# A retention layer with routed experts: past products first, row stores on GpSimd, and the last stores split

## The chip, the cores and the metric

The kernel runs on one core of a Trainium2 chip. The core has five engines that run side by side, each with a queue of its own: TensorE (PE in the profile; PEld is its weight load), VectorE (DVE), ScalarE (ACT), GpSimd (POOL) and SyncE (SP), which here only issues DMAs. Sixteen DMA engines move data between the chip's memory and the core's SBUF. The metric is the device time of one execution in microseconds.

## The reference, cut to what matters

```python
# q, k, v: (8 batches, 8 heads, 576 tokens, 64), float32
scores = scale * q @ k.T
ret = scores * gamma[h] ** (t - s)        # for t >= s, else 0
x = (ret @ v) -> (8, 576, 512)            # heads side by side

logits = x @ w_gate                       # 8 experts
local = sigmoid(x @ w_local)
for b in batches:
    for s in tokens:
        e = argmax(logits[b, s]) if s == 0 or local[b, s] < 0.5 else e of the token before
        out[b, s] = softmax(logits[b, s])[e] * relu(x[b, s] @ w1[e]) @ w2[e]
...
```

The first half is a retention layer: causal attention without a softmax, whose weight decays with the distance. The second sends each token to one of eight experts (512 to 1024 to 512), where a token may take over the expert of the token before it.

## The kernel before, in words

**The retention stage.** The 4608 tokens (two sequences of 576 are nine chunks of 128) are handled in 36 chunks (NCH). A chunk's output has two parts: the products of its own masked scores with its values, and the products of its queries with the state that all earlier chunks of the sequence left. The state is a sum of key-value products, kept in PSUM (kv) and copied to SBUF after every chunk (states, two buffers). The chunk in the middle of a pair of sequences (MID) is half of the one and half of the other; the first chunk of a pair has no past.

The order on TensorE is written by hand (a manual schedule); for one step i of the loop it is: the scores of chunk i+1 (function scores, line 176), the outputs of chunk i (outputs: the value products, line 201, and then the past products, line 210), the state update of chunk i+1 (state, line 227), the gate products of chunk i-1 (rows, line 238), and the logits of chunk i-2 (logits, line 260), followed by a step of the routing when one is open. The other engines take the work in an order that the framework's scheduler chose. These matmuls use different parts of the TensorE array: scores contract over 64 rows into 128 columns (written 64*128), value products 128*64, past products 64*64, state updates 128*64 (64*64 in the middle chunk), gates 128*32, logits 128*128.

What the other engines do for a chunk: SyncE loads q, k and v in one DMA of 1 MB (ld, line 156, seven buffers) and, in between, pieces of the first expert's weights (line 162); DVE scales q (qT, line 165), masks the scores from PSUM into sT (line 180) and transposes the outputs in squares of 32 (x, line 247); POOL scales v (vs, line 169, four buffers) and writes one-hot lanes for the routing (line 187); ACT copies the outputs (xT, line 213), the state (line 230) and the gate products (line 241) out of PSUM. Each two chunks, four DMAs store the rows of x to a scratch tensor in memory (xd, line 250); in the kernel before they are issued by ACT. x has two buffers, each for two chunks. From xd the tokens are gathered later, expert by expert.

**The routing** (route) follows groups of 6 to 8 chunks on DVE and POOL, and ends some 30 us after the last chunk; TensorE fills part of this with tokens of expert 0 that are known early (block(-1)).

**The expert stage.** Tokens are sorted by expert into blocks of up to 768 tokens (GMAX = 6 groups of 128). For block j the function step(j) is run: POOL loads the weights of the next block and gathers its tokens (weights, load_tokens); a switch on the number of tokens (tc.Switch, for PE and ACT) picks one of the compiled variants of block(j, T). A block first does the first group of second-layer products of the block before it (first_group(j-1), line 683), then its own first layer (line 745), then the remainder in narrow pieces of 64 and 32 tokens (narrow), and then its groups 1, 2, 3 and so on (group, line 683, with ACT scaling each result into ys, line 687). Its own group 0 is left to the next step. After the switch POOL stores the results row by row with indirect DMAs (store, line 662): first group 0 of the block before, then groups 1 to 5 and the two narrow pieces (store_rest). A store that has no rows writes none but is still issued. NSURE is 9, so the steps that always run are 0 to 8, and with this data step 7 is the last with a block of its own; step 8 has only the first group of block 7 left, and its store.

Of the kernel before, what the change touches and what calls it, by code (L numbers as in the profile page):

```python
# [18 lines left out]
ET = mybir.EngineType  # L19
# [3 lines left out]
P = 128  # L23
B, H, S, DH = 8, 8, 576, 64
# [3 lines left out]
HP = H // 2  # L28
# [14 lines left out]
GMAX = TMAX // P  # L43
# [3 lines left out]
NSURE = E + 1  # L47

SIZES = [0, P] + list(range(2 * P, TMAX + 1, 32))
# [5 lines left out]
NARROW = (P // 2, P // 4)  # L55
# [7 lines left out]
def kernel(  # L63
# [10 lines left out]
    nc = tc.nc  # L74
# [44 lines left out]
    with ExitStack() as part:  # L119
# [70 lines left out]
        def outputs(i):  # L190
            m = i % PER
            g = chunks[i]
            qT, vs, sT = g["qT"], g["vs"], g["sT"]


            ops = ps_o.tile([P, 2, HP, P], F32, name="ops")
            for c in range(HP):
                for u in range(2):
                    r = slice((u ^ c & 1) * DH, ((u ^ c & 1) + 1) * DH)
                    h = 2 * c + u  # L200
                    nc.tensor.matmul(ops[r, c & 1, c // 2, :], lhsT=vs[:, h * DH:(h + 1) * DH], rhs=sT[:, u, c, :],  # L201
                                     start=(c < 2), stop=(m == 0), skip_group_check=True)
            if m > 0:

                n = HALF if m == MID else P
                for c in range(HP):
                    for u in range(2):
                        k = slice(u * DH, (u + 1) * DH)
                        r = slice((u ^ c & 1) * DH, ((u ^ c & 1) + 1) * DH)
                        nc.tensor.matmul(ops[r, c & 1, c // 2, 0:n], lhsT=states[(i + 1) % 2][k, c, :],  # L210
                                         rhs=qT[k, c, 0:n], start=False, stop=True, skip_group_check=True)
            g["xT"] = xT = work.tile([P, HP, P], F32, name="xT", bufs=2)
            nc.scalar.copy(xT.rearrange("p (a b) t -> p b a t", b=2), ops[:, :, 0:HP // 2])  # L213

# [17 lines left out]
        def rows(i):  # L232
            nonlocal x
            xT = chunks[i]["xT"]

            gps = ps_g.tile([P, P], F32, name="gps")
            for c in range(DK):
                nc.tensor.matmul(gps[c * SQ:(c + 1) * SQ, :], lhsT=gates[:, c, :], rhs=xT[:, c, :],
                                 start=True, stop=True, skip_group_check=True)
            parts = work.tile([P, P], F32, name="parts")  # L240
            nc.scalar.copy(parts, gps)
            chunks[i]["parts"] = parts


            if i % 2 == 0:
                x = work.tile([P, 2, NSQ, DK, SQ], F32, name="x", bufs=2)
            nc.vector.transpose(x[:, i % 2], xT.rearrange("p c (t s) -> p t c s", s=SQ))  # L247
            if i % 2:
                for a in range(NSQ):
                    nc.scalar.dma_start(  # L250
                        out=xd[(i - 1) * P:(i + 1) * P, a * P:(a + 1) * P].rearrange("(t s) d -> s t d", s=SQ),
                        in_=x[a * SQ:(a + 1) * SQ].rearrange("p b t c r -> p (b t) (c r)"))

# [200 lines left out]
        for M, at in ((P // 2, 0), (P // 4, 0), (P // 4, P // 2)):  # L454
            r = repeat[M, at] = table.tile([P, P], F32, name=f"repeat{M}_{at}")
# [12 lines left out]
        with tc.manual_schedule(engines={ET.PE}):  # L468
            for i in range(NCH + 2):
# [9 lines left out]
                if 0 <= i - 2:  # L479
# [3 lines left out]
                    if i - 2 in ends[:-1]:  # L483
                        k = ends.index(i - 2)
# [35 lines left out]
    narrow_ys = {M: later.tile([P, D * M // P], F32, name=f"y{M}") for M in NARROW}  # L520
    rows_of = [later.tile([P, GMAX], I32, name=f"rows{i}") for i in range(2)]
    narrow_rows = [{M: later.tile([P, 1], I32, name=f"rows{M}_{i}") for M in NARROW} for i in range(2)]
# [33 lines left out]
    n = rt.tile([P, E], F32, name="n")  # L556
# [46 lines left out]
    sizes = rt.tile([P, (NBLK + 1)], F32, name="sizes")  # L603
# [4 lines left out]
    kind = rt.tile([P, NBLK + 1], F32, name="kind")  # L608
# [52 lines left out]
    def store(y, rows, n=1):  # L661
        nc.gpsimd.indirect_dma_start(  # L662
            out=next(views).rearrange("t (q d) -> (t q) d", q=n), out_offset=bass.IndirectOffsetOnAxis(ap=rows, axis=0),
            in_=y, in_offset=None, bounds_check=n * NTOK - 1, oob_is_err=False)
# [13 lines left out]
    def group(j, g, between=None):  # L678

        slot, w = (slot_of[j % 3], w2s[j % 2]) if j >= 0 else (slot_soon, w2s[0])  # L680
        yps = next(yps_) if g else yps0[j % 2]
        for m in range(FK):
            nc.tensor.matmul(yps, lhsT=hT[:, m, g * P:(g + 1) * P], rhs=w[:, m, :],  # L683
                             start=(m == 0), stop=(m == FK - 1))
            if between:
                between(m)
        nc.scalar.activation(ys[:, g], yps, Act.Copy, scale=slot.bitcast(F32)[:, g, 1:2])  # L687

    def first_group(j, between=None):
        group(j, 0, between)  # L690
        slot = slot_of[j % 3] if j >= 0 else slot_soon
        nc.scalar.copy(rows_of[(j + 1) % 2][:, 0:1], slot[:, 0, 0:1])
# [19 lines left out]
                                 start=(m == 0), stop=(m == FK - 1), skip_group_check=True)  # L712
        nc.scalar.activation(narrow_ys[M], yps[:, 0:D // n], Act.Copy, scale=share)

    def block(j, T):

        xg = xgs[j % 2]
        w = w1s[max(j, 0) % 2]
        groups = [(g, min(P, T - g * P)) for g in range(-(-T // P))]
        xT = xTs[j % 2]  # L720

        def turn(g, M):
            xps = next(hps_).rearrange("p (c t) -> p c t", c=DK)
            for c in range(DK):
                for a in range(NSQ):
                    at = a * P + c * SQ
                    nc.tensor.matmul(xps[a * SQ:(a + 1) * SQ, c, 0:M], lhsT=xg[0:M, g, at:at + SQ],
                                     rhs=ident[0:M, 0:M], start=True, stop=True, skip_group_check=True)
            nc.scalar.copy(xT[:, :, g * P:g * P + M], xps[:, :, 0:M])  # L729


        if j > 0:
            first_group(j - 1)
        elif j == 0:
            first_group(j - 1, lambda m: turn(*groups[m - 1]) if 1 <= m <= len(groups) else None)
        else:
            for g in groups:
                turn(*g)
        n = -(-T // TN)
        for m in range(FK):  # L740
            for i in range(n):
                cols = slice(i * T // n, (i + 1) * T // n)
                hps = next(hps_)
                for c in range(DK):
                    nc.tensor.matmul(hps[:, 0:T // n], lhsT=w[:, m, c, :], rhs=xT[:, c, cols],  # L745
                                     start=(c == 0), stop=(c == DK - 1))
                nc.scalar.activation(hT[:, m, cols], hps[:, 0:T // n], Act.Relu)  # L747


        first = T // P * P  # L750
        if first > P and j >= 0:
            nc.scalar.copy(rows_of[j % 2][:, 1:first // P], slot_of[j % 3][:, 1:first // P, 0])
        for M in NARROW:
            if T - first >= M:
                narrow(j, first, M)
                first += M
        for g, M in groups[1:]:
            if M == P:
                group(j, g)

    def kind_of(j):
        return nc.values_load(desc[0:1, 0, j:j + 1], engines=[ET.PE, ET.Activation], min_val=0, max_val=len(SIZES),
                              skip_runtime_bounds_check_because="a count of sizes")

    load_tokens(0)
    block(-1, TSOON)
    for g in range(1, TSOON // P):
        store(ys[:, g], slot_soon[:, g, 0:1])

    def load_next(j):  # L770
        weights(j + 1, False)
        load_tokens(j + 1)

    def store_rest(j):
        for g in range(1, GMAX):
            store(ys[:, g], rows_of[j % 2][:, g:g + 1])
        for M in NARROW:
            store(narrow_ys[M], narrow_rows[j % 2][M], P // M)

    def step(j):  # L780


        for rows in (rows_of[j % 2], *narrow_rows[j % 2].values()):
            nc.vector.memset(rows, P // min(NARROW) * NTOK)


        if 0 < j < NBLK:
            weights(j, True)
        if j != NSURE - 1 and j + 1 < NBLK:
            load_next(j)  # L790
        kind = kind_of(j)
        for k in tc.Switch({ET.PE: kind, ET.Activation: kind}, len(SIZES) + 1):
            if k == len(SIZES):
                first_group(j - 1)
            elif SIZES[k] and j < NBLK:
                block(j, SIZES[k])
        store(ys[:, 0], rows_of[j % 2][:, 0:1])
        if j != NSURE - 1:
            store_rest(j)

    with tc.manual_schedule(engines={ET.Pool, ET.DVE}):
        for j in range(NSURE):
            step(j)
# [69 lines left out]
```

## Time and profile before

| | |
|---|---|
| time, median of 3 | 736.68 us (736.45 to 738.42) |
| span of the profiled execution | 732.8 us |
| mean granted TensorE clock | 0.974 |
| PE busy | 688.8 us, 94% |
| PEld busy | 455.2 us, 62% |
| DVE busy | 182.1 us, 25% |
| ACT busy | 145.0 us, 20% |
| POOL busy | 232.9 us, 32% |
| moved by DMA | 116.55 MB, 159 GB/s over the span |

The shares are means over two stages that have little in common. In the first, up to about 170 us, loads, DVE and TensorE are all busy. In the second TensorE alone is. The rows to look at are those of the first stage and of the last 20 us. A line of the timeline or of a group reads: start and length in us (or busy time and mean of one in ns), engine, line of the code, operation, out<-in by the program's names, shape, and in brackets the idle time of the engine before it with what ended it. "issue" means that the profile shows nothing that the engine waited for.

### The profile page before, as it was taken

How to read it: one execution, taken by the hardware profiler on the slowest of the kernel's cores; microseconds unless marked ns; L12 is line 12 of the kernel's file. 1: busy time of each engine (PE TensorE's matmuls, PEld its weight loads, DVE VectorE, ACT ScalarE, POOL GpSimd, SP SyncE). 2: the span in 40 equal slices, each digit the busy share in tenths (PEclk: the TensorE clock that was granted, in tenths of full speed). 3: DMA queues.
4: the chain of work that ended last, by engine and by line, in shares of the span. 5: the costliest groups of instructions: out<-in, count | busy, mean ns of one | idle time of the engine just before them, and what ended most of it. 6: DMA issues, size and time to landing. Idle time of an engine off the chain costs nothing. (4 is left out here: it accounts for less than half of the span.)

```text
span 732.8 us, 12623 instructions
## 1 busy us (share of the span) xinstructions
PE 688.8 (94%) x4960; PEld 455.2 (62%) x4960; DVE 182.1 (25%) x488; ACT 145.0 (20%) x375; POOL 232.9 (32%) x337
## 2 busy tenths in 40 slices
PE   5997999997989999999999999999999999999990
PEld 4876877785734547646754764675487467548640
DVE  5757769887900100200020010002001000200200
ACT  6221222223111112111211110221021112112100
POOL 5232525525270036008102700720270081035013
PEclk9998999997998999999999999999999999999996
DMA  8999999832085018405711740571175067014311
GB/s 336 335 345 356 382 348 339 302 96 51 2 254 116 1 47 303 94 3 206 229 24 62 298 107 3 178 242 33 57 284 128 7 229 199 4 62 140 74 36 49
DMA packets 72013, 116.55 MB, mean 159 GB/s; under 512 B 9160, under 2 KB 52300, under 8 KB 67408
## 3 DMA queue, kind: packets, MB, share of 16 engines
q1 hardware_dynamic: 34688, 54.80, 23.9%
q0 software_dynamic: 17184, 50.36, 18.8%
q10 hardware_dynamic: 20016, 9.82, 4.8%
q8 instruction: 66, 1.08, 0.7%
q14 instruction: 59, 0.48, 0.2%
HBM read 90.82 MB, written 24.12 MB: 157 GB/s over the span
## 5 line engine op out<-in xcount | busy, mean ns | idle before, releaser
L745 PE MATMUL hps<-xT,w1s 128*128 128x304 f32 (+4 forms) x1024 | 258.4, 414 | 0.7 <-ACT xT L729 0.7
L745 PEld LDWEIGHTS hps<-xT,w1s 128*128 128x128 f32 x1024 | 195.6, 191 | 65.0 <-issue 14.0
L683 PE MATMUL yps<-w2s,hT 128*128 128x512 f32 x528 | 232.5, 599 | 1.1 <-issue 1.1
L683 PEld LDWEIGHTS yps<-w2s,hT 128*128 128x128 f32 x528 | 100.0, 191 | 125.2 <-issue 124.9
L662 POOL DMA_INDIRECT out_dram<-ys,rows x49 | 48.8, 996 | 342.1 <-ACT ys L687 329.8
L747 ACT ACTIVATE hT<-hps 128x304 f32<-128x304 f32 (+4 forms) x128 | 53.1, 418 | 202.7 <-PE hps L745 193.7
L655 DVE STREAM_TRANSPOSE xT<-squares 128x512 f32<-128x512 f32 x48 | 29.4, 677 | 198.9 <-PE yps L710 150.7
L644 DVE CAST both<-slot 128x6 f32<-128x6 int32 x9 | 1.6, 172 | 259.0 <-POOL slot L638 259.0
L169 POOL TENSOR_TENSOR vs<-ld,decs 128x512 f32<-128x512 f32 x36 | 39.0, 1086 | 81.2 <-PE ops L201 42.1
L176 PE MATMUL sps<-qT,ld 64*128 64x128 f32 x576 | 49.1, 303 | 14.0 <-DMA ld<-in_qkv_dram 6.8
L640 POOL DMA_INDIRECT xg<-xd,slot x54 | 55.1, 1020 | 19.8 <-issue 13.0
L176 PEld LDWEIGHTS sps<-qT,ld 64*128 64x128 f32 x576 | 40.6, 202 | 17.4 <-DVE sT L180 8.6
L687 ACT ACTIVATE ys<-yps,slot 128x512 f32<-128x512 f32 x31 | 21.3, 688 | 147.3 <-PE yps L683 146.7
L180 DVE TENSOR_TENSOR sT<-sps,mask 128x512 f32<-128x512 f32 x72 | 45.8, 676 | 11.0 <-PE sps L176 10.3
L201 PE MATMUL ops<-sT,vs 128*64 128x128 f32 x576 | 42.4, 291 | 1.8 <-ACT xT L213 0.9
L213 ACT COPY xT<-ops 128x512 f32<-128x512 f32 x36 | 21.1, 587 | 111.4 <-PE ops L210 74.5
L201 PEld LDWEIGHTS ops<-sT,vs 128*64 128x64 f32 x576 | 33.1, 143 | 6.8 <-POOL vs L169 1.2
L165 DVE TENSOR_TENSOR qT<-ld,decq 128x512 f32<-128x512 f32 x36 | 31.4, 876 | 6.9 <-DMA ld<-in_qkv_dram 3.5
L247 DVE STREAM_TRANSPOSE x<-xT 128x512 f32<-128x512 f32 x36 | 25.3, 703 | 22.8 <-DMA xd<-x 18.3
L710 PE MATMUL yps<-w2s,hT 128*32 128x128 f32 (+1 forms) x544 | 30.1, 306 | 0.0
L710 PEld LDWEIGHTS yps<-w2s,hT 128*32 128x32 f32 (+1 forms) x544 | 21.2, 118 | 5.2
L227 PE MATMUL kv<-vs,ld 128*64 128x64 f32 (+1 forms) x512 | 22.5, 232 | 0.6 <-POOL one_of_blk L418 0.6
(194 smaller groups left out, 360.3 us busy)
## 6 DMA issues: line engine op xcount, KB each, us to landing
ld<-in_qkv_dram SPq DMA_DIRECT2D x35, 1024.0 KB, 8.2
w1s<-in_w_dram POOLq DMA_DIRECT2D x32, 512.0 KB
w2s<-in_w_dram POOLq DMA_DIRECT2D x32, 512.0 KB
squares<-xg SPq DMA_DIRECT2D x128, 96.0 KB, 2.3
xd<-x ACTq DMA_DIRECT2D x72, 128.0 KB, 5.3
w1s<-in_w_dram SPq DMA_DIRECT2D x8, 256.0 KB, 7.2
w2s<-in_w_dram SPq DMA_DIRECT2D x8, 256.0 KB, 6.7
ld<-in_qkv_dram SPq DMA_DIRECT2D x4, 256.0 KB, 5.8
```

The costliest lines, as they stand in the source:

```text
L165: nc.vector.tensor_tensor(qT, ld[:, 0].rearrange("p (c s) -> p c s", c=HP), decq[:, m], op=Alu.mult)
L169: scaled = nc.gpsimd.tensor_tensor(vs.rearrange("p (h d) -> p h d", h=H), vn.rearrange("p (h d) -> p h d", h=H), deck[:, m, :].unsqueeze(2 ...
L176: nc.tensor.matmul(sps[u][:, c, :], lhsT=kT[r, c, :], rhs=qT[r, c, :], start=True, stop=True, skip_group_check=True)
L180: nc.vector.tensor_tensor(sT[:, u], sps[u], (mask2 if m == MID else mask).unsqueeze(1).to_broadcast([P, HP, P]), op=Alu.mult)
L201: nc.tensor.matmul(ops[r, c & 1, c // 2, :], lhsT=vs[:, h * DH:(h + 1) * DH], rhs=sT[:, u, c, :], start=(c < 2), stop=(m == 0), skip_group ...
L640: nc.gpsimd.indirect_dma_start(out=xgs[j % 2][:, g, :], out_offset=None, in_=xd, in_offset=bass.IndirectOffsetOnAxis(ap=slot[:, g, 0:1], a ...
L655: nc.vector.transpose(xTs[j % 2][:, :, g * P:(g + 1) * P].rearrange("p c (t s) -> p t c s", s=SQ), squares[:, g].rearrange("p t (c r) -> p ...
L662: nc.gpsimd.indirect_dma_start(out=next(views).rearrange("t (q d) -> (t q) d", q=n), out_offset=bass.IndirectOffsetOnAxis(ap=rows, axis=0) ...
L683: nc.tensor.matmul(yps, lhsT=hT[:, m, g * P:(g + 1) * P], rhs=w[:, m, :], start=(m == 0), stop=(m == FK - 1))
L710: nc.tensor.matmul(yps[q * M:(q + 1) * M, 0:D // n], lhsT=hT[:, m, first:first + M], rhs=w[:, m, q * D // n:(q + 1) * D // n], start=(m == ...
L745: nc.tensor.matmul(hps[:, 0:T // n], lhsT=w[:, m, c, :], rhs=xT[:, c, cols], start=(c == 0), stop=(c == DK - 1))
L747: nc.scalar.activation(hT[:, m, cols], hps[:, 0:T // n], Act.Relu)
```

## The change

Three parts. The past products of a chunk are put ahead of the value products, so that the value products (128*64) stand next to the state update (128*64); the flags that begin and end accumulation in PSUM move with them. The four row stores of each two chunks are issued by GpSimd instead of ACT. And in the last step that has a block, the work of the block is split over two switches: the second holds only group 1, and POOL stores all other results between the two; in all steps the narrow pieces are now stored ahead of the groups.

```diff
             ops = ps_o.tile([P, 2, HP, P], F32, name="ops")
-            for c in range(HP):
-                for u in range(2):
-                    r = slice((u ^ c & 1) * DH, ((u ^ c & 1) + 1) * DH)
-                    h = 2 * c + u
-                    nc.tensor.matmul(ops[r, c & 1, c // 2, :], lhsT=vs[:, h * DH:(h + 1) * DH], rhs=sT[:, u, c, :],
-                                     start=(c < 2), stop=(m == 0), skip_group_check=True)
             if m > 0:
...
                         nc.tensor.matmul(ops[r, c & 1, c // 2, 0:n], lhsT=states[(i + 1) % 2][k, c, :],
-                                         rhs=qT[k, c, 0:n], start=False, stop=True, skip_group_check=True)
+                                         rhs=qT[k, c, 0:n], start=(c < 2), stop=False, skip_group_check=True)
+            for c in range(HP):
+                for u in range(2):
...
+                    nc.tensor.matmul(ops[r, c & 1, c // 2, :], lhsT=vs[:, h * DH:(h + 1) * DH], rhs=sT[:, u, c, :],
+                                     start=(m == 0 and c < 2), stop=True, skip_group_check=True)
...
                 for a in range(NSQ):
-                    nc.scalar.dma_start(
+                    nc.gpsimd.dma_start(
                         out=xd[(i - 1) * P:(i + 1) * P, a * P:(a + 1) * P].rearrange("(t s) d -> s t d", s=SQ),
...
-    def block(j, T):
+    def block(j, T, part=None):
...
+        if part == 1:
+            if groups[1:] and groups[1][1] == P:
+                group(j, 1)
+            return
...
-        for g, M in groups[1:]:
+        for g, M in groups[1 if part is None else 2:]:
             if M == P:
                 group(j, g)
...
-    def store_rest(j):
-        for g in range(1, GMAX):
+    def store_rest(j, groups=range(1, GMAX), sizes=NARROW):
+        for M in sizes:
+            store(narrow_ys[M], narrow_rows[j % 2][M], P // M)
+        for g in groups:
             store(ys[:, g], rows_of[j % 2][:, g:g + 1])
-        for M in NARROW:
-            store(narrow_ys[M], narrow_rows[j % 2][M], P // M)
...
+        apart = j == NSURE - 2
         for k in tc.Switch({ET.PE: kind, ET.Activation: kind}, len(SIZES) + 1):
             if k == len(SIZES):
                 first_group(j - 1)
             elif SIZES[k] and j < NBLK:
-                block(j, SIZES[k])
+                block(j, SIZES[k], 0 if apart else None)
         store(ys[:, 0], rows_of[j % 2][:, 0:1])
-        if j != NSURE - 1:
+        if apart:
+            store_rest(j, range(2, GMAX))
+            for k in tc.Switch({ET.PE: kind, ET.Activation: kind}, len(SIZES) + 1):
+                if k < len(SIZES) and SIZES[k]:
+                    block(j, SIZES[k], 1)
+            store_rest(j, (1,), ())
+        elif j != NSURE - 1:
             store_rest(j)
```

More of the change, by code (lines that the diff above doesn't have):

```diff
@@ L210, in outputs @@
                         nc.tensor.matmul(ops[r, c & 1, c // 2, 0:n], lhsT=states[(i + 1) % 2][k, c, :],
-                                         rhs=qT[k, c, 0:n], start=False, stop=True, skip_group_check=True)
+                                         rhs=qT[k, c, 0:n], start=(c < 2), stop=False, skip_group_check=True)
+            for c in range(HP):
+                for u in range(2):
+                    r = slice((u ^ c & 1) * DH, ((u ^ c & 1) + 1) * DH)
+                    h = 2 * c + u
+                    nc.tensor.matmul(ops[r, c & 1, c // 2, :], lhsT=vs[:, h * DH:(h + 1) * DH], rhs=sT[:, u, c, :],
+                                     start=(m == 0 and c < 2), stop=True, skip_group_check=True)
             g["xT"] = xT = work.tile([P, HP, P], F32, name="xT", bufs=2)
```

## The prediction

> **What bounds the kernel now.** I read the slices of the page first (PE at 8 to 9 tenths everywhere, the DMA engines at 8 to 9 tenths only up to about 150 us), then the window sums of the first stage and of the rest.
>
> ```profile
> 23.25:163.30 140.05, 131.10 (x2335) 106.85 (x2331) 106.10 (x251) 36.04 (x103) 54.49 (x76) 0.98 0.89 312
> 172.00:733.00 561.00, 535.87 (x2357) 330.74 (x2357) 59.75 (x203) 92.69 (x233) 162.60 (x207) 0.97 0.37 114
> ```
>
> The columns are length, then busy time of PE, PEld, DVE, ACT and POOL, then granted clock, DMA share and GB/s. The expert stage (second line) is plain TensorE work: 536 of 561 us. The change touches it only at its very end. The retention stage (first line: from the scores of chunk 3 to those of chunk 35, so 32 chunks in 140.05 us, 4.38 us each) has PE, DVE (106 us) and the DMA engines (0.89, and 0.97 to 1.02 between 40 and 140 us) all near their limit, POOL at only 54.5 us. So I look there for what ends the waits. The timeline of PE shows the beat:
>
> ```profile
> 46.30 1.16 PE L176 MATMUL sps<-qT,ld 64*128 64x128 f32 x16
> 50.31 1.70 PE L176 MATMUL sps<-qT,ld 64*128 64x128 f32 x16
> 59.01 2.67 PE L176 MATMUL sps<-qT,ld 64*128 64x128 f32 x16 [4.84 <-DVE sT L180]
> 65.30 1.16 PE L176 MATMUL sps<-qT,ld 64*128 64x128 f32 x16
> ```
>
> An undisturbed chunk takes 50.31 - 46.30 = 4.01 us. Two in nine are 0.6 us shorter (no past product, or no state update). 32 chunks would take 32 x 4.01 - 7 x 0.6 = 124 us, so 16 us of the 140 are disturbance. The timeline of DVE tells what the 4.84 us were:
>
> ```profile
> 51.07 0.69 DVE L165 TENSOR_TENSOR qT<-ld,decq 128x512 f32<-128x512 f32 x1 [0.27 <-DMA ld<-in_qkv_dram]
> 57.07 0.71 DVE L247 STREAM_TRANSPOSE x<-xT 128x512 f32<-128x512 f32 x1 [5.31 <-DMA xd<-x]
> 58.28 1.28 DVE L180 TENSOR_TENSOR sT<-sps,mask 128x512 f32<-128x512 f32 x2
> ```
>
> The transpose wants an x buffer whose store has not landed; the masked scores queue behind it on DVE, and PE behind those. The stores' own line says 1.9/5.3/13.5 us (least, median, most) from issue to landing. The loads suffer from the same stores; the waits of the SyncE queue:
>
> ```profile
> SPq L156 <- DMA xd<-x: 36.7, 8, 8.9
> SPq L162 <- DMA xd<-x: 34.5, 9, 10.9
> SPq L156 <- PE kv L227: 18.1, 7, 5.0
> ```
>
> A load of q, k and v has no data to wait for from an x store. What they share is DMA semaphores: in the records ACT's stores and SyncE's loads take turns on the same ten (100 to 109), and the load of 56.91 us waits for semaphore 104, last given to the store issued at 43.44 and landed at 56.90. GpSimd's own DMAs use another set (111 to 118).
>
> [...]
>
> ```profile
> q0 software_dynamic: 17184, 50.36, 18.8%
> q10 hardware_dynamic: 20016, 9.82, 4.8%
> ```
>
> Packets of ACT's queue average 491 bytes (512-byte rows, one a packet), of GpSimd's 2931 bytes, though its gathers have 2 KB rows. A store of one pair is 1024 packets of 512 bytes[...]. [...]
>
> ```profile
> 118.77 0.42 PEld L210 LDWEIGHTS ops<-qT,state 64*64 64x64 f32 x16 [0.17 <-issue]
> 119.37 0.55 PEld L227 LDWEIGHTS kv<-vs,ld 128*64 128x64 f32 x16 [0.17 <-issue]
> 109.36 0.61 PEld L227 LDWEIGHTS kv<-vs,ld 64*64 64x64 f32 x16
> ```
>
> 128*64 to 64*64 and back costs 0.17 us each; where the update is 64*64 too (third line) there is no gap.
>
> **The change part by part.**
> 1. Order of the output products. Today scores (64*128), values (128*64), past (64*64), update (128*64); after it scores, past, values, update: one change of mode less. 27 chunks have both a past product and a full update and gain up to 0.17 us; the 4 chunks in the middle of a sequence pair (update 64*64) lose as much. Net at most 23 x 0.17 = 3.9 us, and only while PE ends the chunk. Half of it: 2 us. The state that now comes first was copied a whole iteration before, so no new wait there. The value products end where the past products ended, so the copy to xT comes no later; vs is freed about 0.6 us later, against a lead of up to three chunks.
> 2. Stores by GpSimd. Removed: the disturbance of 50.31 to 65.30 (14.99 us instead of 7.4, of it some through the halved clock after the idle stretch: granted 0.77 there), 7.6 us; that of 96.18 to 111.82 (three periods, 15.64 instead of 12.0, with DVE waits of 3.97 and 2.54 us on stores), 3.6 us. Of the other 4.8 us, about half is ACT held up at its own store issues (72 of 0.43 us median, and xT or lt waiting behind them): 2.4 us. Sum 13.6, with the order of part 1 15.6 us.
>    Added: 72 issues on POOL. This form (32 partitions, 8 rows of 512 bytes each, 256 descriptors) isn't in the trace. The nearest row:
>
> ```profile
> L674 POOL DMA_DIRECT2D w1s<-in_w_dram x32: 8/588/642, 200.6 to 662.4; - x32
> ```
>
>    128 descriptors of 4 KB in 588 ns, following each other every 0.52 us (the shortest are skipped loads). Bounds: 0.55 us if the issue is the price, 1.3 us if twice the descriptors plus the 0.30 us that POOL idles between indirect DMAs. I take 1.05. In the stage 64 of them are 67 us, and POOL goes from 54.5 to 122 us: it fits in 128, but with little air, and the in-order queue puts each vs (line 169) behind four stores that wait for DVE's transposes. vs has four buffers, so bursts of 4.2 us are mostly bridged.
>    Given back: at 4.0 us a chunk 1.05 MB of load, 0.26 of store and 0.13 of weights are 360 GB/s; 60 to 80 us reached 376, 100 to 140 us only 331 to 339 at a share of 0.99. POOL and DMA together: I give back 5.6 of the 15.6 us. Stage: 10 us.
>    After the loop the last logits (line 265) waited 1.71 us behind the last four store issues on ACT; the routing chain on DVE and the first gathers hang on them. 1 us, as the last x stores now take POOL's time instead.
> 3. The last-but-one step. Now:
>
> ```profile
> 709.27 0.69 ACT L687 ACTIVATE ys<-yps,slot 128x512 f32<-128x512 f32 x1 [6.18 <-PE yps L683]
> 710.24 1.02 POOL L662 DMA_INDIRECT out_dram<-ys,rows  x1 [36.63 <-ACT ys L687]
> 716.14 0.69 ACT L687 ACTIVATE ys<-yps,slot 128x512 f32<-128x512 f32 x1 [0.48 <-PE yps L683]
> 719.34 0.98 POOL L662 DMA_INDIRECT out_dram<-y,rows  x1
> 720.63 0.98 POOL L662 DMA_INDIRECT out_dram<-ys,rows  x1 [0.30 <-issue]
> ```
>
>    Eight stores of 1.30 us start when the whole block is done; the last product is ready at 716.83, but its store stands ninth, at 720.63. After it: the first part ends one group earlier (709.27 - 6.87 = 702.40), its seven stores run from 703.4 to 712.5, group 1's to 713.5, and the last goes at 716.83 + 0.28 = 717.1: 3.5 us earlier, and the end of the program follows it at a fixed distance. The second switch costs ACT about 5.5 us (709.96 to 715.47 today), inside the 6.87 us of a group; PE's queue had its next group ready today without a gap. I cost it at nothing.
>
> Sum: 10 + 1 + 3.5 = 14.5 us; 736.7 - 14.5 = 722 us.
>
> **The rivals.**
> - POOL becomes the bound. For it: 122 of 128 us is tight, stores wait in order, the price is a guess. Against: 42.1 us of POOL's idle time is waiting for PE to free vs, so it has lead. At 1.3 us a store 54.5 + 83 = 138 us, with some waiting in order 145: 5 us longer than now, less 4.5 for the end: about 737; at 1.5 us 745. Slower or the same. Chance 0.19.
> - The transfers stay the bound: stores land sooner, but at the cost of loads. For it: 0.99 share at 335 GB/s. Against: nothing says that loads were late but for those held by semaphores. Half of the stage's gain: 5 + 4.5, 727 to 731 us. Chance 0.23.
> - All 15.6 us come, with the whole 1.7 of ACT and the 3.5 of the end: 736.7 - 20.8 = 716 us. Chance 0.12.
> - The forecast, 717 to 727 us: 0.46.
>
> **How the numbers follow.** The range reaches from just under the third case (713) to the mild form of the first (738), leaving about 0.17 out. Faster by over 2.2 us: the forecast, the second and third and nearly nothing of the first, 0.80; the first splits into 0.07 within 0.3% and 0.13 slower.
>
> **What would show it.** Right: no DVE wait of line 247 on xd stores above 1 us, no SyncE wait on them; landing of stores near 4 us; chunks of about 4.05 us; line 227 without its 0.17 us gap; the last store about 0.3 us behind the last ys. Wrong: POOL over 95% busy between 25 and 150 us with PE or DVE waiting for vs (line 169); stores above 1.2 us each; line 169 slowed; a gap on PE at the second switch.

## The result and the profile after

| | before | after |
|---|---|---|
| time, median | 737.24 us (736.45 to 738.42) | 727.89 us (725.35 to 731.44) |
| ratio, 95% interval | | 0.9875 (0.9829 to 0.9922) |
| span of the profiled execution | 732.8 us | 727.2 us |
| scores of chunk 35 start | 163.30 | 154.15 |
| last logits copy, lt (line 265) | 172.04 | 161.58 |
| block 0's first W1 product | 227.44 | 216.63 |
| last ys of block 7 | 716.14 | 710.32 |
| last store issued | 720.63 | 711.29 |
| from there to the end of the span | 12.2 us | 15.9 us |

The median is 9.35 us lower. (In the experiments further down a few executions, of 736 to 739 us where the kernel before takes 730.7, were in a slower state with a lower granted clock, 0.956 to 0.969 where the medians of the others were 0.973 to 0.978; the ratios and the mean clocks leave them out.) The table is read downwards by the differences between its two columns: 9.2, 10.5, 10.8, then only 5.8, then 9.3, and at the end 5.6. By block 0's first product the changed kernel is nearly 11 us ahead. It loses 5.0 us of that before the last ys and 3.7 us after the last store, and wins 3.5 us between the two.

The window sums of the changed kernel, over the same two stretches (scores of chunk 3 to scores of chunk 35, and the expert stage; columns as before):

```profile
19.15:154.15 135.00, 129.75 (x2335) 108.63 (x2332) 109.52 (x251) 36.35 (x103) 96.06 (x141) 0.96 0.88 332
162.00:727.00 565.00, 532.00 (x2357) 328.36 (x2350) 58.62 (x203) 92.43 (x232) 166.72 (x216) 0.98 0.37 114
```

The 32 chunks take 135.0 us instead of 140.05, and at a lower clock: 0.96 granted against 0.98. POOL has 96 us of work instead of 54.5, far from the 135 it could hold. The waits of DVE for the stores' landing (total, times, longest, in us), before and then after:

```profile
DVE x L247 <- DMA xd<-x: 18.3, 9, 5.3
```

```profile
DVE x L247 <- ACT xT L213: 8.2, 13, 1.9
...
DVE x L247 <- DMA xd<-x: 3.3, 2, 2.5
```

And the waits of the SyncE queue after:

```profile
SPq L156 <- PE kv L227: 87.7, 26, 8.2
SPq L156 <- PE sps L176: 3.8, 3, 1.5
```

DVE waited 18.3 us for x stores to land; 3.3 us are left. SyncE waited 71 us for them and now waits for none: its loads are ahead, and what they wait for most, 87.7 us, is line 227, which reads a loaded chunk and so frees its buffer. As far as the profiles show, the stores do not land sooner on the whole. The profile after shows no landing of a store; those of e2, e4, e5 and e6 below, which have the same stores on GpSimd, show 19 of the 72, with a median of 6.5 to 6.6 us and the longest at 7.8 to 8.4 us. Before, of the 44 that the profile shows, the median was 5.3 us and the longest 13.5 us. What went are the long landings. The page's rows of the stores, of the scaling next to them in POOL's queue, and of the DMA queues:

```profile
q0 software_dynamic: 20640, 59.80, 23.2%
...
q10 hardware_dynamic: 432, 0.38, 0.2%
...
L169 POOL TENSOR_TENSOR vs<-ld,decs 128x512 f32<-128x512 f32 x36 | 41.4, 1158 | 27.6 <-issue 10.5
...
L250 POOL DMA_DIRECT2D xd<-x x72 | 42.6, 599 | 14.6 <-DVE x L247 6.7
```

ACT's queue lost 19584 packets, and GpSimd's gained only 3456 for the same 9.44 MB: 2731 bytes each instead of 482. In the records 18432 packets of 512 bytes became 2304 of 4096, so 32 a store where there had been 256; the other 1152, 16 a store, have 4 bytes in both. A store costs POOL 599 ns. The past products' weight load, followed by that of the value products and of the state update, in one chunk:

```profile
67.40 0.32 PEld L204 LDWEIGHTS ops<-qT,state 64*64 64x64 f32 x16
67.79 0.85 PEld L210 LDWEIGHTS ops<-sT,vs 128*64 128x64 f32 x16
68.61 0.60 PEld L227 LDWEIGHTS kv<-vs,ld 128*64 128x64 f32 x16
```

The gap of 0.17 us ahead of line 227 is gone. So it is in 26 of the 30 chunks that have both value products and an update behind them; in the other four, the middle ones with the 64*64 update, 0.17 us now stands there, as the prediction said. And the last two groups of block 7, in the timeline:

```profile
691.60 0.69 ACT L687 ACTIVATE ys<-yps,slot 128x512 f32<-128x512 f32 x1 [6.18 <-PE yps L683]
...
692.35 7.13 PE L683 MATMUL yps<-w2s,hT 128*128 128x512 f32 x16 [0.78 <-ACT ys L687]
...
699.64 0.69 ACT L687 ACTIVATE ys<-yps,slot 128x512 f32<-128x512 f32 x1 [7.35 <-DMA out_dram<-ys,rows]
...
701.49 8.80 PE L683 MATMUL yps<-w2s,hT 128*128 128x512 f32 x16 [2.01 <-issue]
...
710.32 0.69 ACT L687 ACTIVATE ys<-yps,slot 128x512 f32<-128x512 f32 x1 [3.88 <-PE yps L683]
711.29 0.98 POOL L662 DMA_INDIRECT out_dram<-ys,rows  x1 [7.29 <-ACT ys L687]
```

The last store is issued 0.97 us behind the start of the last ys instead of 4.49: 3.5 us won. But from the ys two groups earlier to the last one it takes 710.32 - 691.60 = 18.72 us instead of 13.73: PE stood idle for 0.78 and 2.01 us and then ran a group, which takes 6.87 us at full clock, in 8.80 us, as its clock was halved for 3.4 us from 702.9 on. That makes 5.0 us lost.

### The profile page after: what moved, and what is told of

Read it like the earlier page. It is cut to its first block, busy times and chain, and to the rows that moved or that the text cites. A ratio compares the mean times of both kernels' runs of the same rounds, so it can differ in the third digit from the quotient of the medians.

```text
span 727.2 us, 12650 instructions
## 1 busy us (share of the span) xinstructions
PE 680.1 (94%) x4960; PEld 451.9 (62%) x4960; DVE 184.6 (25%) x488; ACT 145.1 (20%) x375; POOL 277.2 (38%) x409
## 5 line engine op out<-in xcount | busy, mean ns | idle before, releaser
L176 PE MATMUL sps<-qT,ld 64*128 64x128 f32 x576 | 47.0, 297 | 10.1 <-DVE past L318 6.3
L169 POOL TENSOR_TENSOR vs<-ld,decs 128x512 f32<-128x512 f32 x36 | 41.4, 1158 | 27.6 <-issue 10.5
L250 POOL DMA_DIRECT2D xd<-x x72 | 42.6, 599 | 14.6 <-DVE x L247 6.7
L176 PEld LDWEIGHTS sps<-qT,ld 64*128 64x128 f32 x576 | 39.1, 198 | 13.0 <-DVE past L318 6.3
L710 PEld LDWEIGHTS yps<-w2s,hT 128*32 128x32 f32 (+1 forms) x544 | 21.2, 118 | 5.2
```

The costliest lines, as they stand in the source:

```text
L169: scaled = nc.gpsimd.tensor_tensor(vs.rearrange("p (h d) -> p h d", h=H), vn.rearrange("p (h d) -> p h d", h=H), deck[:, m, :].unsqueeze(2 ...
L176: nc.tensor.matmul(sps[u][:, c, :], lhsT=kT[r, c, :], rhs=qT[r, c, :], start=True, stop=True, skip_group_check=True)
L250: nc.gpsimd.dma_start(out=xd[(i - 1) * P:(i + 1) * P, a * P:(a + 1) * P].rearrange("(t s) d -> s t d", s=SQ), in_=x[a * SQ:(a + 1) * SQ].r ...
L710: nc.tensor.matmul(yps[q * M:(q + 1) * M, 0:D // n], lhsT=hT[:, m, first:first + M], rhs=w[:, m, q * D // n:(q + 1) * D // n], start=(m == ...
```

## The experiments

Each is compared with the kernel before on the same chip. There were three chips: the first for e1 to e4, the second for e5 to e8, the third for e9 to e12. The kernel before took 730.7, 729.9 and 736.7 us on them, so the ratios are what counts, and a difference between ratios of two chips is less sure than one within a chip.

### The parts one by one

**e1**: only the products' order changed (the diff of function outputs alone). 

> Part 1 alone: the past products first, the stores on ACT and one switch as before. My theory (the stores' move made the gain): 0 to 2 us below before, since SyncE and DVE keep their waits on the x stores and the chunks' period in the quiet stretches falls by only 0.1 to 0.17 us. Rival (the order made the gain): 8 us or more below before.

**e2**: only the stores' engine.

```diff
-                    nc.scalar.dma_start(
+                    nc.gpsimd.dma_start(
                         out=xd[...
```

> Part 2 alone: the x stores on GpSimd, the products in the old order, one switch. My theory: 8 to 11 us below before, the waits of SyncE and DVE on x gone, the scores of chunk 35 some 7 to 9 us earlier; the end after the last store as long as in the changed kernel (near 15.9 us against 12.2), because it carries the same 72 more GpSimd transfers. Rival (the end's length is chance): the end takes near 12.2 us again.

**e3**: only the second switch and the order of the stores around it. 

> Part 3 alone: only the last-but-one step's stores are split. My theory: the last store comes 3.5 us closer behind the last group's activation, and PE loses about 5 us at the second switch, so the time is 1 to 2 us above before. Rival (the prediction's step): 3.5 us below before.

**e4**: the changed kernel without that switch. 

> Parts 1 and 2 without part 3. My theory: 1 to 2 us below the changed kernel, near 726 us against its 727.9, with the last group's products at 6.9 us, no 5 us lost at a second switch, and a last store some 4.5 us behind the last activation. Rival (the prediction's step: the split is worth 3.5 us): 3.5 us above it, near 731.

**e5**: the changed kernel once more. 

> The changed kernel again, beside the other runs of this call. Theory: 1 to 2 us above the run without the split (0.9929 of before), so 0.994 to 0.996 of before. Rival (the split gives its 3.5 us): 0.988 of before.

| | median us | ratio to before | 95% interval |
|---|---|---|---|
| e1 order | 730.58 | 0.9997 | 0.9970 to 1.0024 |
| e2 stores on GpSimd | 723.54 | 0.9911 | 0.9876 to 0.9946 |
| e3 split | 729.78 | 0.9991 | 0.9969 to 1.0014 |
| e4 order and stores | 725.39 | 0.9929 | 0.9902 to 0.9957 |
| e5 all three | 722.78 | 0.9899 | 0.9856 to 0.9942 |

The stores' engine alone makes a gain of the size of the whole; the order and the split, each alone, make no measurable difference. For the split together with the other parts the runs do not decide. The expected loss of 1 to 2 us was not met: e5's 0.9899 is nearer to the rival's 0.988, and e4 lies 0.3 to 0.5% above the two measurements of all three parts (0.9875 and 0.9899), but on other chips and with intervals that overlap. In the profiles PE loses 5.0 us (the first profile), 5.2 us (e3) and 3.1 us (e5) around the split, and the last store wins 3.5 us in each. So the split comes out even at best: from the third last ys to the end of the span e4 takes 33.55 us and e5 33.52. In e5 the clock was not halved there; in the other two it was, for 3.4 us.

Why is the order worth nothing? In the quiet stretches chunks do start every 3.85 us in e1, e4 and e5 instead of 4.00, which over 32 chunks would be 4.8 us. But the profiles have stretches in which the clock is halved, here 3.4 or 6.8 us long. Window sums of the retention stage, e1 first, then e2:

```profile
19.80:168.44 148.64, 133.18 (x2336) 110.71 (x2332) 101.17 (x251) 35.23 (x103) 56.73 (x76) 0.95 0.87 303
```

```profile
20.11:150.94 130.83, 127.50 (x2336) 104.29 (x2332) 108.44 (x251) 37.77 (x103) 96.32 (x141) 1.00 0.90 342
```

In this stage e1 was granted 0.95 of the clock and e2 all of it. Over the executions, and with the standard error, the mean clock of the whole program was 0.9714 (0.0010) in e1 against 0.9736 (0.0006) before, and 0.9734 (0.0012) in e4 against 0.9767 (0.0015) in e2. Neither difference is twice its error or more. By estimate 0.002 to 0.003 of 730 us is 1.5 to 2.2 us of full clock, so less than half of the 4.8 us is accounted for.

### Was it DVE's wait or the shared semaphores?

**e8** leaves the stores on ACT and gives x four buffers, so that DVE never has to wait for a landing; the loads still share semaphores with the stores (before, the records give the DMAs of both engines the same eight: 100, 102 to 106, 108 and 109; the page counts their packets apart, the loads' in q1 and the stores' in q10).

```diff
-        raw = pool(part, "raw", 7)
+        raw = pool(part, "raw", 6)
...
-                x = work.tile([P, 2, NSQ, DK, SQ], F32, name="x", bufs=2)
+                x = work.tile([P, 2, NSQ, DK, SQ], F32, name="x", bufs=4)
```

> The kernel before with four x buffers in place of two and, to make room, six load buffers in place of seven: stores still on ACT. It takes away DVE's wait for a store's landing and leaves the stores in the queues that the loads use. Theory (the loads' wait on the stores' completions and the slow stores matter more than DVE's wait): SyncE still waits for x stores in all some 50 us or more, the scores of chunk 35 stay within 3 us of before's range (163 to 169), and the time is within 3 us of before. Rival (DVE's wait for the landing was what counted): DVE's wait goes, chunk 35's scores come 8 us or more earlier, and the time falls by 4 us or more.

Measured 722.76 us, ratio 0.9896 (0.9859 to 0.9933): as fast as the whole change, which took 722.78 us on the same chip (e5). My theory fell, and the rival held in the time; the scores of chunk 35 came at 157.56 us, 5.7 us before those of the kernel before (163.30) and not the 8 it named. The SyncE queue still waits for the stores, and it hardly matters:

```profile
SPq L156 <- DMA xd<-x: 38.3, 10, 9.1
...
SPq L162 <- DMA xd<-x: 30.5, 9, 4.0
```

DVE's waits for the stores' landing at line 247 are gone (21.2 us, six times, in e1). The stage's window:

```profile
19.51:157.56 138.05, 131.67 (x2336) 107.35 (x2332) 106.99 (x251) 36.35 (x103) 57.19 (x77) 0.96 0.93 327
```

To compare stages I take off half of the halved stretches that the clock's records show in each (an estimate, as PE is busy in most of that time). Stores on ACT: 140.05 - 3.4 = 136.6 before, 148.64 - 6.8 = 141.8 in e1, 145.63 - 8.5 = 137.1 in e3. Four x buffers: 138.05 - 5.1 = 132.9. Stores on GpSimd: 130.8 in e2, 127.7 in e4, 129.9 and 129.5 in the two profiles of all parts. By the means, of some 9 us between stores on ACT and on GpSimd, 5 to 6 are DVE's wait for landings; this is rough, as the three with stores on ACT differ by 5 us among themselves. The rest goes with the move to another queue, and no run separates what in that queue it is. That e8 is nevertheless as fast fits what the move to GpSimd costs elsewhere, in the next two sections.

**e12**: e8 with the past products first. 

> As e8 (stores on ACT, four x buffers, six load buffers), with the past products first. Theory: quiet chunks at 3.85 us instead of 4.00, the time within 2 us of e8's 0.9896 of before, as the loads' wait on the stores and the clock take the difference. Rival (the order is worth 4.8 us): 0.983 of before.

 Measured 728.17 us, ratio 0.9867 (0.9834 to 0.9899), on the third chip. That is 2.1 us below e8's ratio, at the edge of the theory's 2 us. The rival's 0.983 lies just outside e12's interval, but e8's ratio, from another chip, has an interval as wide, so a gain of 4.8 us is not excluded by these two.

### The first cost of the move: what stands behind the last stores

Between the last lt copy and block 0's first W1 product the profiles of the first two chips show two lengths: with the stores on ACT 47.4 us (e1), 47.7 (e3) and 47.2 (e8), with the stores on GpSimd 52.0 (e2), 53.6 (e4) and 52.0 (e5). (e6 and e7, below, take 57.2 and 56.5.) PE in e1, then in e2:

```profile
184.71 13.02 PE L745 MATMUL hps<-xT,w1s 128*128 128x256 f32 x50 [0.69 <-ACT xT L729]
198.53 3.59 PE L108 MATMUL places<-w1s,lanes 128*128 128x220 bf16 x36 [0.80 <-DVE first L573]
201.96 3.20 PE L745 MATMUL hps<-xT,w1s 128*128 128x256 f32 x14
```

```profile
170.84 5.60 PE L745 MATMUL hps<-xT,w1s 128*128 128x256 f32 x14 [7.44 <-ACT xT L729]
178.23 3.58 PE L108 MATMUL places<-w1s,lanes 128*128 128x220 bf16 x36 [1.78 <-DVE first L573]
181.65 10.97 PE L745 MATMUL hps<-xT,w1s 128*128 128x256 f32 x50
```

With the stores on GpSimd the framework's scheduler put block -1's xT copies on ACT behind the lanes of the last routing group (lines 362 and 363) and only 14 instead of 50 of block -1's products ahead of the places products (line 108, the routing's matmuls with the one-hot lanes). So ACT copies xT 11.1 us after lt instead of 4.0, PE stands 7.4 us, and the 36 products that were moved behind the places products stand in the way later. In part this is forced: the copies also wait for the last x stores to land (6.80 us of ACT's idle time in e6 ends with a landing of xd<-x), since xT lies in memory that x held, and POOL issues the last of these 4.9 us after lt, where ACT had issued it 0.5 us before lt. In e6 and e9, where nothing else holds them, the copies start 8.1 and 8.0 us after lt.

**e6** tried to restore the order by giving the last group's lanes to GpSimd.

```diff
-            if i0 == starts[-1]:
...
-                    nc.scalar.activation(far, numbers, Act.Abs, bias=minus[:, k:k + 1])
-                    nc.scalar.activation(lanes[:, i0 + k], far, Act.Relu, bias=1.0, scale=-1.0)
-            else:
...
+            for k in range(i0, i0 + Q):
+                to_lanes.append(partial(nc.gpsimd.tensor_scalar, lanes[:, k], numbers, lane_all[:, k:k + 1],
+                                        None, Alu.is_equal))
```

> Parts 1 and 2 without the split, and the last routing group's lanes are written by GpSimd like all others, so that ACT has nothing ahead of block -1's two xT copies. Theory (4.6 to 6.2 us of the stores' gain were lost because ACT waits for the routing before it copies xT): PE's idle time before block -1's first W1 product falls from about 7 us to under 2, from the last logits copy (lt) to block 0's first W1 product it takes about 48 us instead of 53.6, and the time is 3 to 6 us below the run without the split (near 0.986 of before). Rival (something else, the routing on DVE or the desc, sets block 0): 53 us again and no gain.

728.95 us, ratio 0.9993 (0.9964 to 1.0022): above e4's 0.9929. PE and POOL in the timeline of e6:

```profile
166.07 0.60 POOL L487 TENSOR_SCALAR lanes<-numbers,lane_all 128x128 bf16<-128x128 f32 x1
...
167.69 7.98 PE L736 MATMUL hps<-xT,w1s 128*128 128x256 f32 x22 [4.33 <-ACT xT L720]
...
170.59 3.79 POOL L487 TENSOR_SCALAR lanes<-numbers,lane_all 128x128 bf16<-128x128 f32 x1
...
180.21 2.99 POOL L540 TENSOR_TENSOR w1s<-where,pieces 128x1584 bf16<-128x1584 bf16 x1
...
183.25 5.56 PE L108 MATMUL places<-w1s,lanes 128*128 128x220 bf16 x36 [7.58 <-DVE its_n L588]
```

The first W1 product does come earlier, 9.3 us after lt. But a lane write that takes POOL 0.60 us took up to 3.79 us while DVE ran its large bf16 products (166.8 to 176.5); the write of 3.79 us, from 170.59 on, stands beside two of them (line 540, 170.47 to 173.99). Why it took longer there, no run shows. POOL's own part of the values (line 540) ended at 183.2, and the places products had to wait for it: from lt to block 0, 57.2 us.

**e9** writes the order out instead: block -1's transposes and xT copies are emitted ahead of the last routing, its first products ahead of the places products, and the lanes on ACT are held behind the copies.

```diff
+    for g in range(TSOON // P):
+        turned = turn(-1, g, P)
+
     for step in (*routing, route(starts[-1], GROUPS[-1], lt)):
...
+    first_layer(-1, TSOON)
...
+                    with tc.issue_after(turned.ins):
+                        nc.scalar.activation(far, numbers, Act.Abs, bias=minus[:, k:k + 1])
```

> Parts 1 and 2 without the split, and block -1's two xT copies and its first products stand ahead of the last routing group's lanes on ACT and of the 36 places products on PE. Theory (the stores' move turned this order round, and 4.6 to 6.2 us were lost by it): PE's idle time between the last logits products and the end of the places products falls from about 10 us to under 4, from the last lt copy to block 0's first W1 product it takes 47 to 49 us instead of 52 to 53.6, and the time is 4 to 5 us below the run without the split: 0.986 to 0.988 of before. Rival (the routing on DVE sets block 0 whatever PE does in between): 52 us again.

728.98 us, ratio 0.9880 (0.9848 to 0.9912), as the theory expected, but e4's 0.9929 came from another chip, and the length from lt to block 0 is 57.2 us, not the 47 to 49 expected. PE's order is right (64 products, then places without a gap), and then PE stalls in block 0's transposes:

```profile
204.82 0.33 PE L525 MATMUL hps<-ident,xg 128*32 128x128 f32 x2 [0.94 <-issue]
205.57 0.27 PE L525 MATMUL hps<-ident,xg 128*32 128x128 f32 x1 [0.43 <-issue]
206.29 0.40 PE L525 MATMUL hps<-ident,xg 128*32 128x128 f32 x3 [0.45 <-issue]
207.73 0.43 PE L525 MATMUL hps<-ident,xg 128*32 128x128 f32 x2 [1.04 <-issue]
```

These gaps, with nothing that the profile shows to wait for, come to 3.5 to 5.1 us in the four profiles of the third chip, and to 3.6 and 2.0 us in those of the kernel before and after at the head of this document; in the profiles of the first two chips there are none inside the transposes. In e9 the clock is halved there too, from 207.1 for 10.2 us.

The gaps and the clock hide what the order does. To see it, I take off the gaps, and half of the time in which the clock was halved and PE busy (an estimate from one profile each, in us):

| | stores on | lt to block 0 | halved, PE busy | gaps | left |
|---|---|---|---|---|---|
| e1 | ACT | 47.4 | 8.2 | 0 | 43.3 |
| before | ACT | 55.4 | 13.8 | 3.6 | 44.9 |
| e12 | ACT | 55.4 | 14.2 | 3.5 | 44.8 |
| e2 | GpSimd | 52.0 | 4.7 | 0 | 49.7 |
| after | GpSimd | 55.1 | 3.2 | 2.0 | 51.5 |
| e9 | GpSimd, order written out | 57.2 | 10.7 | 5.0 | 46.8 |

So the changed order costs some 6.5 us on either kind of chip, and e9 gives 3 to 5 of them back; about 2 remain against e12, which has the stores on ACT and the same chip, and the forced wait of the copies can account for them. That the profiles before and after take the same time there does not mean that the order is free: the one before had more gaps and more halved clock. What causes the gaps, and whether they or the waits set off the halved clock, is not shown.

**e10**: e9 with the products in the old order. 

> As e9, with the products in the old order. Theory (the new order saves 0.15 us a chunk at full clock and gives it back in halved-clock time): quiet chunks take 4.00 us instead of 3.85, the mean granted clock over the runs is 0.003 higher than e9's, and the time is within 2 us of e9's. Rival (the order is worth 32 x 0.15 = 4.8 us): 4 to 5 us above e9.

 730.84 us, ratio 0.9899 (0.9864 to 0.9933), 1.9 us above e9 (728.98), so within the theory's 2 us, at its edge. The mean clock is 0.9717 (0.0011) against 0.9698 (0.0007), a difference of 0.002 and not the 0.003 expected. In all three pairs the new order has the lower clock, though in none of them by twice the error.

### The second cost of the move: the end of the program

After the last store has landed GpSimd's queue does two more long things, an increment of its transfers' semaphores and a drain; the program ends 1.18 us after the drain in the kernel before and 0.84 us after it in the changed one. From the traces' records:

```
kernel    transfers by GpSimd   increment ns   drain ns
before    186                   1627           5957
e11       226                   1792           6604
e4        258                   2352           8891
after     258                   2352           8891
e7        330                   2392           9060
```

In e1, e3, e8 and e12, with 186 transfers, the drain takes 5957 ns too, and in e2, e5, e6, e9 and e10, with 258, it takes 8891. So with the 72 stores on GpSimd the end is longer by 2.93 + 0.73 = 3.66 us. It is not chance, as the rival in e2's expectation had it. (In e3's profile the increment starts some 1.8 us later behind the last store than in the others, for a reason that stays open.)

**e7** doubles the number, with each x store in two halves.

```diff
                 for a in range(NSQ):
-                    nc.gpsimd.dma_start(
+                    for b in range(2):
+                        nc.gpsimd.dma_start(
...
```

> Parts 1 and 2 without the split, each x store in two halves: 144 stores of 128 rows in place of 72 of 256, the same bytes and packets, 72 more GpSimd transfers (330 against 258). Theory (each GpSimd transfer costs the end of the program 40.7 ns of drain and 10 ns of semaphore work): the drain takes 8.89 + 2.93 = 11.8 us and the step before it 2.35 + 0.73 = 3.1 us. If the price of a store is its issue and not its rows, one half takes 0.58 us too, and GpSimd then has some 20 of each 20 us to do in the retention stage, which slows it. Rival: the drain stays at 8.9 us, and a half store takes 0.3 us.

The drain grew by only 0.17 us: a fixed price for each transfer is refuted. The other half held: a store of 128 rows took 561 ns against 599 for 256, so its price is nearly all in the issue. POOL in 20 to 60 us, in e7 and then in e4 (busy time, instructions, clock, DMA share, GB/s):

```profile
20.00:40.00 20.00, 17.33 (x27) 1.00 1.02 413
40.00:60.00 20.00, 16.64 (x24) 0.91 1.02 414
```

```profile
20.00:40.00 20.00, 12.62 (x17) 1.00 1.02 414
40.00:60.00 20.00, 13.03 (x16) 1.00 1.02 412
```

Even so POOL is not full, and the stage takes 138.71 - 6.8 = 131.9 us, 4 us more than e4's 127.7. There is one execution of e7 alone, of 735.4 us, so its time is not compared with others. From lt to block 0 it takes 56.5 us, with PE idle for 11.8 us until ACT copies xT.

**e11** takes transfers away: e9 with the weights in halves.

```diff
-        for m in range(0, FK, 2):
+        for m in range(0, FK, 4):
...
-                out=to[:, m:m + 2].rearrange("p m d -> p (m d)"),
+                out=to[:, m:m + 4].rearrange("p m d -> p (m d)"),
```

> As e9, with each expert's weights in two transfers of four slices in place of four of two: 32 fewer GpSimd transfers (226 against 258), the same bytes. Theory (up to about 262 transfers each costs the end 40.7 + 10.1 ns): the drain takes 5.96 + 40 x 0.0407 = 7.59 us and the step before it 1.63 + 40 x 0.0101 = 2.03 us, so 1.6 us less than in e9, and the time is 1 to 2 us below e9. Rival (the drain doesn't follow the number): 8.9 or 6.0 us.

725.91 us, ratio 0.9819 (0.9781 to 0.9856), 3.1 us below e9 on the same chip and the lowest ratio of all; last store to end 12.1 us against e9's 15.6. The end shrank by 2.85 us in those two steps, more than the 1.6 expected. What sets their length is open: above the first row the drain and the increment grow together, four to one, in all the other rows, so both seem to follow the same thing, but it isn't the plain number of transfers.

## Why the prediction came out as it did

The forecast was 722.0 us (713 to 738); the measured 727.89 lies inside the range, 5.9 us above the forecast and just outside the 717 to 727 of its main case.

- **The stage (10 us) and lt (1 us).** Chunk 35 came 9.15 us earlier and lt 10.46 us: right in size. DVE's wait of line 247 on landings fell to 3.3 us, SyncE's went, stores cost 0.60 us, under the 1.05 taken and close to the lower bound, and POOL had 39 us to spare. The reason was only half right. I gave the shared semaphores and the small packets as much weight as DVE's wait. That small packets make a store land late or hold up a load was my assumption, and no run tests it alone. e8, with the same 512-byte rows stored by ACT, shows that DVE's wait alone is 5 to 6 of some 9 us of the stage, with SyncE's waits still there. (The load at 56.91 us, the prediction's example, is a piece of weights, line 162; loads of q, k and v waited as well. The shared semaphores are eight, not ten.)
- **The signs.** Three of those named for "right" did not come: the longest wait of DVE is 2.5 us and not under 1; the stores land in 6.5 to 6.6 us by the median (in e2, e4, e5 and e6) and not near 4; a chunk takes 135.0 / 32 = 4.22 us on the mean and not 4.05. SyncE's waits and the gap ahead of line 227 went, and the last store is 0.28 us behind the end of the last ys, as forecast. Of the signs of being wrong, the gap on PE at the second switch came, and line 169 was slowed a little (1158 ns on the mean instead of 1086).
- **The order (2 us).** The gap is gone and a quiet chunk is 0.15 us shorter, near the 0.17 I took. The times of e1 against before, e4 against e2, e9 against e10 and e12 against e8 give -0.2, +1.9, -1.9 and, by their ratios, -2.1 us: from 2 us gained to 2 us lost, with no direction that is sure. The clock was lower in each of the three pairs of one chip; that a denser PE causes this is argued, not shown.
- **The split (3.5 us) is the step that failed.** The stores' side was exact: 4.49 to 0.97 us. "I cost it at nothing" was wrong for PE. PE takes the second switch too, stands idle 2.8 us around it (0.78 + 2.01) and loses 3.1 to 5.2 us in all. I had looked at ACT's 5.5 us alone and taken PE's gapless queue at one switch for that at two. e3 measures the part alone at 0.9991 (0.9969 to 1.0014), not the 0.995 that 3.5 us would be. Beside the other parts, e4 against the two measurements of the whole leaves room for a gain of 2 to 4 us, which the profiles do not show.
- **"The end of the program follows it at a fixed distance" failed as well**: 12.2 us became 15.9, 3.66 of it in the drain and the increment. No row of the page shows these two, and I had not asked the records what stands between the last store and the end.
- **The changed order of ACT's and PE's work in front of block 0** was no step of the prediction at all. It costs some 6.5 us by the estimate above.
- **The rivals.** POOL as the bound fell; with twice the stores (e7) it reached 17.3 of 20 us and the stage grew by 4 us. The transfers as the bound fell too: 409 to 413 GB/s between 20 and 60 us in the changed kernel, against 334 to 335 before, and SyncE waits 87.7 us for free buffers, so that loads were not late. The time that this rival named, 727 to 731 us, was met by another way: the stage gave its gain and the end took the rest.

Of the 14.5 us summed, 3.5 for the split and 3.7 for the end are missing, which leaves 7.3, against 5.6 in the profiles and 9.35 in the medians. That the number is this near is in part luck: the cost in front of block 0, which nobody had forecast, does not appear in the pair of profiles because the profile before lost about as much there by gaps and halved clock.

## What to carry to other kernels

When an engine waits for a store to land and other work stands behind that wait (here up to 5.3 us on DVE, with PE behind it), try more buffers before another queue: here four x buffers, paid for with one load buffer, brought what the move brought (722.76 us, where the whole change took 722.78 on the same chip), without its costs. Both together were not tried. A second switch cost PE time here (3.1 to 5.2 us in three profiles) as well as ACT, so look at the queue of each engine that takes a switch, not only at the one whose work is in question. A part moved to another engine may turn the scheduler's order elsewhere (some 6.5 us here, by estimate) and lengthen the program's end (3.66 us here); subtract the two profiles at marks all along the program, not only where the change is, and look at the clock between the marks before you trust a difference.

## What the runs showed of the hardware

- A plain transfer cost GpSimd nearly the same in the three shapes that were run: 561 ns for a store of 128 rows (e7), 599 ns for 256 (after), 588 ns by the median for a weight load of 128 rows (before).
- Stores of 512-byte rows went out in packets of 512 bytes when ACT issued them (18432 of them, before) and of 4096 bytes when GpSimd did (2304, after).
- With the stores on GpSimd the median landing was no shorter (6.5 to 6.6 us against 5.3), but the longest was (7.8 to 8.4 us against 13.5).
- The drain near the end of the program took 5.96, 6.60, 8.89 and 9.06 us with 186, 226, 258 and 330 GpSimd transfers; it had the same length to the ns in every profile with the same number.
- PE lost 3.5 to 5.1 us in transposes with nothing to wait for on one chip, and nothing on two others. The same kernel takes 6 to 7 us longer on that chip; how much of that is due to these gaps was not measured.
- A GpSimd operation of 0.60 us took 3.79 us beside DVE's bf16 products (e6); the cause was not shown.
